# Moving ScalarE's first shifted copy ahead of the second unit's exponentials, with half the constant turns

## The chip, the cores and the metric

The kernel runs on one core of a Trainium2 chip. The metric is the time of one execution in microseconds (us), lower is better. A core has TensorE (PE in the profile, with PEld for its weight loads), VectorE (DVE), ScalarE (ACT), GpSimd (POOL) and SyncE (SP), which here only issues transfers.

## The reference

Sliding-window causal attention with a window of 64 over 8 batches, 8 heads, 576 positions and 64 dimensions a head, in float32, is followed by a mixture of 8 experts in which the expert of a token depends on the token before it.

```python
scores = scale * q @ k.T                      # mask: 0 <= pos_q - pos_k < 64
attn = softmax(where(mask, scores, -1e9))
x = (attn @ v) as [8, 576, 512]
# per token: fresh = argmax(x @ w_gate); gate = sigmoid(x @ w_local)
# e = fresh if first or gate < 0.5 else the expert of the token before
# out = softmax(logits)[e] * relu(x @ w1[e]) @ w2[e]
```

## The kernel before

The 4608 tokens are taken in 9 groups (`sc`) of 512 and each group in 4 head pairs (`hp`): a **unit** is one group and one head pair, and there are 36. The attention of all units comes first, up to about 131 us in the profile; then come the experts, with the matrix products of blocks of 256 tokens, up to the end. Between them, and partly beside the attention, the router's tables are built.

For a unit, `scores` (L378) makes 36 small matmuls into two PSUM tiles `sp` (each a weight load and a matmul of 64x128 from `w`, the tile of q and k; L385), then two exponentials on ScalarE into the SBUF tile `p` (L416), then one multiplication of `p` with a mask on VectorE (L421). `values` (L423) makes 32 matmuls from `p` with the value tiles `va` and `vb` into a PSUM pair `xo` (L431), and then VectorE takes a reciprocal (L436) and writes the scaled result `x` (L441). `sp` has three buffers, so the tiles of units 1, 2, 3, 4, 5 take buffers (0,1), (2,0), (1,2), (0,1), (2,0). `xo` has two pairs, used in turn.

`va` holds the values as they come from memory; `vb` holds them shifted by 64 rows, because windows cross the blocks of 128. For the first group `shift_first` (L369) makes `vb`, four heads at a time: GpSimd copies the lower rows (L375), ScalarE the upper ones (L376). Both need the transfer of that half of `va`. For later groups `shift` (L355) does the same in four steps (L360 to L367).

`warm(n)` (L245) puts n turns (transposes of the constant identity matrix) on TensorE, into a PSUM bank that nobody reads (L249). It stands twice: 12 turns at the start and 24 between the scores of the first two units and the values of the first.

The orders of TensorE, ScalarE and SyncE are the order in which the program is written (`manual_schedule`). VectorE's and GpSimd's are chosen ahead of time by a planner in the framework, with constraints such as `issue_after`, which holds the second mask's construction (`build_mask(1)`, L275) behind the multiplication that was traced last. All waits are semaphores that the framework places.

The start runs so: scores of units 1 and 2; `shift_first(0)`; the turns; then in the loop for i = 0 the values of unit 1, the scores of unit 3, `shift_first(1)`; for i = 1 the values of unit 2 and the scores of unit 4; for i = 2 the scores of unit 5 (the second group's first) and the values of unit 3; and so on, scores two units ahead. At i = 3 also eight turns of the first group's result, for the router (`turn`, L302).

The transfers of the second group (`load(1, ...)`, L228 and L233) are issued on SyncE behind `until(0, ...)` (L239), a tiny transfer that waits for the first mask; those of the third group behind a like one that waits for unit 1's reciprocal.

Of the kernel before, what the change touches and what calls it, by code (L numbers as in the profile page):

```python
# [83 lines left out]
def kernel(  # L84
# [37 lines left out]
    with ExitStack() as fast:  # L122
        ring = fast.enter_context(tc.tile_pool(name="ring", bufs=4))
        rt = Router(fast, tc, lt, xs, tabs, ident)
        ex = Experts(fast, tc, ring, *moe)
        zeros, n = ex.xp.tile([P, PITCH], F32, name="xg"), (ZR - T1) // HF
        nc.vector.memset(zeros[:HF], 0.0)
        for i in (ZR, N + 1):
            nc.gpsimd.dma_start(out=xs[i:i + 1, :], in_=zeros[:1])
        nc.gpsimd.dma_start(out=xs[T1:ZR, D:].rearrange("(c p) o -> p c o", p=HF),  # L130
                            in_=zeros[:HF, :n * (PITCH - D)].rearrange("p (c o) -> p c o", c=n))
        attention(tc, ring, kq, v3, v4, vt, vh, xs, lt, ok, wgs, wg2s, ident, rt, ex)
        ex.run(fast, rt, lambda ps: flag(nc, ps, ok, bad, tabs["ej"][:, NBLK:], rare, ident))
# [34 lines left out]
def attention(ctx, tc, ring, kq, v3, v4, vt, vh, xs, lt, ok, wg, wg2, ident, rt, ex):  # L168
# [31 lines left out]
    def bank():  # L200

        return ps_e.tile([P, SC], F32, name="r")
# [8 lines left out]
    def space(name, sc):  # L211
        return kp.tile([P, 4, H, width(sc)], F32, name=name, bufs=2 if name == "vb" else 3)
# [24 lines left out]
    def until(i, x):  # L237

        nc.sync.dma_start(out=late[:, i:i + 1], in_=x)  # L239
# [5 lines left out]
    def warm(n):  # L245

        r = bank()
        for _ in range(n):
            nc.tensor.transpose(r[:, :P], ident, ident)  # L249
# [20 lines left out]
    def build_mask(i):  # L270
        m = cp.tile([P, KB, 2, WIN], F32, name=f"mask{i}")
        for c in range(2):
            h = slice(c * WIN, (c + 1) * WIN)
            for par in range(2):
                nc.vector.tensor_scalar(m[h, :, par, :], colf[h], rowf[h], None, Alu.is_ge if par == c else Alu.is_lt)  # L275
        mid = MID[i]
        other = slice((1 - mid % 2) * WIN, (2 - mid % 2) * WIN)
        nc.vector.memset(m[other, mid // 2, mid % 2, :], 0.0)
        masks.append(m.rearrange("p a b q -> p (a b q)"))
# [89 lines left out]
    def shift_first(half):  # L369

        va, h = vas[0], slice(4 * half, 4 * half + 4)
        if not half:
            vbs[0] = space("vb", 0)
            nc.gpsimd.memset(vbs[0][WIN:, 0], 0.0)
        nc.gpsimd.tensor_copy(vbs[0][:WIN, :, h], va[:WIN, :, h])  # L375
        nc.scalar.copy(vbs[0][WIN:, 1:, h], va[WIN:, :3, h])  # L376
# [67 lines left out]
    units = [(sc, hp) for sc in range(NSC) for hp in range(HP)]  # L444
    ps = {}
    masked = []
    for u in units[:LEAD]:
        ps[u] = scores(*u)
    shift_first(0)
    with tc.issue_after(masked[-1].ins):  # L450
        build_mask(1)
    warm(24)
    until(0, masks[0][:1, :1])
    load(1, [pairs[0], whole, pairs[1]])
    moves, gated, turned, old = (), None, None, None
# [1152 lines left out]
```

## Time and profile before

| | |
|---|---|
| runs | 645.85, 646.2, 647.71 us; median 646.2 |
| profiled execution | 643.61 us, of it a span of 641.5 us and 2.1 us around it |
| TensorE, matmuls / weight loads busy in the span | 96% / 85% |
| VectorE / ScalarE / GpSimd busy | 63% / 31% / 20% |
| transfers | 166.43 MB; mean busy share of the DMA engines 0.75 to 1.02 by stretches of the first 60 us |
| TensorE idle, 0 to 160 us / 160 to 600 us | 16.8 us / 1.8 us |

The idle times of the last row are worked out from the table of stretches (length less the matmuls' busy time). Times are counted from the start of the span. A matmul's duration in the profile is longer than the distance to the next one, since they overlap: 32 matmuls of 0.22 us take 1.05 us together. In the idle column, a name behind the arrow is what the engine waited for by the profile; "issue" is a wait for nothing that the profile shows.

### The profile page before, as it was taken

The numbers are of one execution on the slowest core, as the hardware profiler recorded it, in microseconds if no ns is written. First come the engines' busy times: TensorE is split into PE (matmuls) and PEld (weight loads), VectorE is DVE, ScalarE is ACT, GpSimd is POOL, SyncE is SP. The second block draws the span as 40 slices with busy tenths as digits, with TensorE's granted clock in tenths as the row PEclk, the third lists the DMA queues.
The fourth block names the chain that finished last, engine by engine and source line by source line (L and its number), as shares of the span: only waits on it lengthen the run. The fifth ranks groups of instructions, "written<-read, shape, count | busy, mean of one in ns | idle before, by whom it ended". The sixth has DMA issues, their size and how long they took to land. (4 is left out here: it accounts for less than half of the span.)

```text
span 641.5 us, 14988 instructions
## 1 busy us (share of the span) xinstructions
PE 616.2 (96%) x6367; PEld 543.7 (85%) x6367; DVE 401.2 (63%) x752; ACT 200.9 (31%) x368; POOL 130.0 (20%) x132
## 2 busy tenths in 40 slices
PE   8888898989999999999999999999999999999995
PEld 7777766878889999978998999887997998899994
DVE  5676488879977775273553683363827653876730
ACT  3756655622572122112120313021211221122120
POOL 5322111330103202102312220221312022101101
PEclk9999999999999999999999999999999999999999
DMA  8988999989746655686957666679768556946501
GB/s 332 417 334 334 377 352 361 342 286 340 242 155 229 242 198 197 214 318 239 395 200 271 220 231 230 238 255 347 266 229 317 206 198 221 389 161 221 218 17 38
DMA packets 29318, 166.43 MB, mean 259 GB/s; under 512 B 8451, under 2 KB 9497, under 8 KB 20026
## 3 DMA queue, kind: packets, MB, share of 16 engines
q1 hardware_dynamic: 20394, 135.54, 58.2%
q0 software_dynamic: 8848, 29.85, 12.1%
q8 instruction: 52, 0.85, 0.5%
q14 instruction: 24, 0.20, 0.1%
HBM read 146.18 MB, written 19.59 MB: 258 GB/s over the span
## 5 line engine op out<-in xcount | busy, mean ns | idle before, releaser
L1387 POOL DMA_INDIRECT out_dram<-y,idx x36 | 42.4, 1178 | 344.3 <-DVE y L1323 196.8
L1314 PE MATMUL hp<-ws,hs 128*128 128x256 f32 x384 | 88.7, 380 | 0.0
L1314 PEld LDWEIGHTS hp<-ws,hs 128*128 128x128 f32 x384 | 72.6, 190 | 10.5 <-issue 0.8
L1264 PE MATMUL hp<-xs,ws 128*128 128x128 f32 x672 | 79.6, 275 | 0.0
L1264 PEld LDWEIGHTS hp<-xs,ws 128*128 128x128 f32 x672 | 77.3, 192 | 0.0
L1323 DVE SCALAR_TENSOR_TENSOR y<-hp,xg,kept 128x256 f32<-128x256 f32 x48 | 22.7, 482 | 74.9 <-issue 47.4
L1407 PE MATMUL hp<-xt,w 128*64 128x64 f32 (+2 forms) x640 | 66.2, 276 | 0.0
L1407 PEld LDWEIGHTS hp<-xt,w 128*128 128x128 f32 (+1 forms) x640 | 60.8, 170 | 4.1 <-issue 0.7
L1314 PE MATMUL hp<-w,h 128*128 128x256 f32 x256 | 61.1, 382 | 0.0
L1275 DVE TENSOR_TENSOR h<-hp,keep 128x512 f32<-128x512 f32 x42 | 28.7, 690 | 48.4 <-PE hp L1264 48.4
L1159 POOL DMA_INDIRECT xg<-xs,gx x40 | 48.2, 1204 | 42.5 <-issue 36.2
L1264 PEld LDWEIGHTS hp<-xt,w 128*128 128x128 f32 x448 | 53.2, 192 | 2.7 <-issue 1.3
L1264 PE MATMUL hp<-xt,w 128*128 128x128 f32 x448 | 54.7, 275 | 0.0
L1314 PEld LDWEIGHTS hp<-w,h 128*128 128x128 f32 x256 | 47.2, 190 | 6.3 <-issue 0.4
L416 ACT ACTIVATE p<-sp 128x512 f32<-128x512 f32 x72 | 39.2, 595 | 38.2 <-PE sp L385 36.1
L431 PE MATMUL xo<-vb,p 128*64 128x74 f32 (+1 forms) x576 | 44.2, 228 | 7.1 <-issue 4.0
L385 PEld LDWEIGHTS sp<-w 64*64 64x64 f32 x1296 | 38.5, 135 | 14.2 <-issue 10.8
L421 DVE TENSOR_TENSOR p<-p,mask 128x1024 f32<-128x1024 f32 x29 | 36.1, 1243 | 20.2 <-ACT p L416 20.1
L385 PE MATMUL sp<-w 64*64 64x128 f32 (+1 forms) x1296 | 44.0, 267 | 4.2 <-issue 3.5
L431 PEld LDWEIGHTS xo<-vb,p 128*64 128x64 f32 x576 | 38.4, 136 | 10.2 <-issue 5.3
L1276 ACT ACTIVATE h<-h 128x512 f32<-128x512 f32 x42 | 26.3, 630 | 59.1 <-DVE h L1275 59.1
L431 PE MATMUL xo<-va,p 128*64 128x74 f32 (+1 forms) x576 | 44.3, 228 | 0.2 <-issue 0.2
(280 smaller groups left out, 951.5 us busy)
## 6 DMA issues: line engine op xcount, KB each, us to landing
w<-in_w_dram SPq DMA_DIRECT2D x42, 2048.0 KB, 8.9
w<-in_kq_dram SPq DMA_DIRECT2D x17, 1024.0 KB, 9.8
w<-in_w_dram SPq DMA_DIRECT2D x24, 512.0 KB, 8.2
xs<-x POOLq DMA_DIRECT2D x9, 1024.0 KB, 11.4
va<-in_v_dram SPq DMA_DIRECT2D x5, 1184.0 KB
vtt<-in_vt_dram SPq DMA_DIRECT2D x5, 1024.0 KB
va<-in_v_dram SPq DMA_DIRECT2D x3, 1040.0 KB, 9.9
va<-in_v_dram SPq DMA_DIRECT2D x2, 520.0 KB, 7.7
```

Of the source, the lines that this page charges most:

```text
L385: nc.tensor.matmul(sp[j][c * WIN:(c + 1) * WIN, a:b], lhsT=kt[h, hp, block * WIN:(block + 1) * WIN], rhs=qt[h, hp, a:b], start=not biased, ...
L416: nc.scalar.activation(p[:, j], sp[j], Act.Exp, scale=DH ** -0.5)
L421: masked.append(nc.vector.tensor_tensor(p, p, m.to_broadcast([P, 2, SC]), op=Alu.mult))
L431: nc.tensor.matmul(xo[par * WIN:(par + 1) * WIN, j, s * VW:s * VW + n], lhsT=p[:, j, b * WIN:(b + 1) * WIN], rhs=w[:, s, 2 * hp + j, :n], ...
L1159: self.nc.gpsimd.indirect_dma_start(out=x, out_offset=None, in_=self.xs[:rows, :], in_offset=bass.IndirectOffsetOnAxis(ap=gx[:, s:s + 1], ...
L1264: nc.tensor.matmul(out[:, m, :], lhsT=a[:, kk, m * P:(m + 1) * P], rhs=b[:, kk, :], start=start and m + kk == 0, stop=stop and (m, kk) == ...
L1275: nc.vector.tensor_tensor(o, x, y, op=add)
L1276: nc.scalar.activation(o, x if y is None else o, Act.Relu)
L1314: nc.tensor.matmul(out, lhsT=a[:, m, :], rhs=b[:, m, :], start=start and m == 0, stop=stop and m == FK // 2 - 1, skip_group_check=True)
L1323: nc.vector.scalar_tensor_tensor(y[i][:, j * w:(j + 1) * w], x, pw[i], y2, Alu.mult, Alu.add)
L1387: self.nc.gpsimd.indirect_dma_start(out=self.out[:, :], out_offset=bass.IndirectOffsetOnAxis(ap=st["idx"][:, s:s + 1], axis=0), in_=y, in_ ...
L1407: nc.tensor.matmul(hp[a, i, :], lhsT=st["w1"][:, kk, m * P:(m + 1) * P][:, a], rhs=st["xt"][:, kk, :n], start=(kk == 0), stop=(kk == DK - 1))
```

## The change

ScalarE's order is changed: the copy of `shift_first(0)` is issued right after the first unit's two exponentials and ahead of the second unit's. GpSimd's two instructions of the same function are traced earlier too. On TensorE the second row of turns has 12 instead of 24 of them; every later TensorE instruction thus stands 24 records (12 weight loads and 12 matmuls) earlier in its stream.

```diff
     for u in units[:LEAD]:
         ps[u] = scores(*u)
-    shift_first(0)
+        if u == units[0]:
+            shift_first(0)
     with tc.issue_after(masked[-1].ins):
         build_mask(1)
-    warm(24)
+    warm(12)
     until(0, masks[0][:1, :1])
     load(1, [pairs[0], whole, pairs[1]])
```

## The prediction

> **What bounds the kernel now.** The engine table first: TensorE's matmuls are busy for 616 of 641.5 us. The table of stretches then says where the other 25 us lie: in 220 to 600 us TensorE idles 0.95 us of 380, but in 0 to 140 us it idles 16.8. So a saving counts only if TensorE is still early where the attention ends (131 us); from there its work is gapless and hands the lead to the end.
>
> The timelines of the engines around the change, TensorE's two lines first, then ScalarE, GpSimd and VectorE:
>
> ```profile
> 9.10 2.84 PE L249 MATMUL r<-ident 128*128 128x128 f32 x24
> 11.87 0.27 PE L431 MATMUL xo<-vb,p 128*64 128x65 f32 x1
> ...
> 9.23 1.09 ACT L416 ACTIVATE p<-sp 128x512 f32<-128x512 f32 x2 [0.73 <-PE sp L385]
> 10.34 0.84 ACT L376 COPY vb<-va 64x780 f32<-64x780 f32 x1
> ...
> 9.51 1.14 POOL L375 COPY vb<-va 64x1040 f32<-64x1040 f32 x1 [3.46 <-DMA va<-in_v_dram]
> ...
> 10.35 1.39 DVE L421 TENSOR_TENSOR p<-p,mask 128x1024 f32<-128x1024 f32 x1 [0.60 <-ACT p L416]
> 11.66 1.79 DVE L275 TENSOR_SCALAR mask<-p,rowf 64x512 f32<-64x512 f32 x4
> ```
>
> Unit 1's values start at 11.87, when the 24 turns end. Their inputs were there at 11.18 (ScalarE's copy, which stood behind unit 2's exponentials), 10.65 (GpSimd's copy) and 9.75 (unit 1's mask). So the turns bind by 0.7 us, behind them the copy.
>
> What TensorE meets next, and later in the attention:
>
> ```profile
> 16.35 0.40 PE L385 MATMUL sp<-w 64*64 64x128 f32 x2 [0.16 <-DMA w<-in_kq_dram]
> 16.92 1.11 PE L385 MATMUL sp<-w 64*64 64x128 f32 x34 [0.17 <-ACT p L416]
> ...
> 28.05 0.99 PE L385 MATMUL sp<-w 64*64 64x128 f32 x24 [0.69 <-issue]
> ...
> 39.70 0.27 PE L385 MATMUL sp<-w 64*64 64x64 f32 x2 [0.83 <-issue]
> ...
> 130.14 0.22 PE L431 MATMUL xo<-vb,p 128*64 128x74 f32 x1 [1.75 <-issue]
> ```
>
> Two walls. At 16.35 unit 5's scores wait for their q and k. And the "issue" pauses are regular: counted from the start of the trace, TensorE's records (loads, matmuls, semaphores) resume after a pause at numbers 705, 961, 1217, 1473, 1729, 1985, 3009, 4033 and 5313, that is 705 plus multiples of 256. The page's queue table has the cause:
>
> ```profile
> q8 instruction: 52, 0.85, 0.5%
> ```
>
> The columns are packets, MB and share of the engines. 0.85 MB in 52 is 16 KB, or 256 records of 64 bytes. In the trace such a transfer starts some 2.4 us before each of these resumptions (25.67 for the one at 28.05).
>
> [...] while the DMA engines are full, the transfer starts 3.3 to 4.7 us after a block was entered (in one case 1.25), and with the 2.4 us a block lasts no less than about 5.7 to 7.1 us: 21.05, 28.05, 33.97, 39.70, 46.81, 53.19 us. [...] the copy waited behind both exponentials though its input was there. [...] The 12 first turns took 2.82 us and the later 24 took 2.84, so the clock was up by 9.1; pauses of 1.75 us did not lower it.
>
> **The change part by part.**
> *The copy.* Its input lands at 9.5 by GpSimd's start. It runs 9.5 to 10.35 (0.84) instead of 10.34 to 11.18. Nothing bounds the landing from below but the end of unit 1's exponentials, 8.5; from above it has no bound: each us that it comes later is a us for unit 2's exponentials, which now stand behind it.
> *The turns.* 12 x (2.84/24) = 1.42 us, 9.10 to 10.52. Unit 1's values then wait for GpSimd's copy alone: 10.65, start 10.7. TensorE gains 11.87 - 10.7 = **1.17 us** here.
> *What is queued behind the moved copy.* Unit 2's exponentials go from 9.23 to 10.37 and end at 11.46 (+1.14). Their PSUM buffers are wanted by unit 3's scores at 11.85: free in time. Unit 2's mask runs 11.5 to 12.7; unit 2's values want it at 12.9: in time. VectorE's queue slips with it: second mask to 14.6, unit 1's reciprocal 14.6 (13.55 before), x to 15.5, unit 3's mask 15.5 (15.26 before, where VectorE had idled 0.84). So VectorE gives back all but 0.25 us, and at 19.26, after another idle 0.65, the rest. SyncE's third-group transfers follow unit 1's reciprocal, 1.1 us later; the DMA engines are at 1.02 of full up to 16 us and 1.01 up to 24, and of 6.2 MB issued for the first two groups about 5.1 have moved at 15.4 (256, 395 and 421 GB/s over 8, 4 and 3.4 us). With 1.1 MB queued they land no later: cost nothing. If that backlog were gone it would be 1.1 us on a transfer whose first reader is unit 9. GpSimd's copy keeps its time.
> *TensorE to the first wall.* Values 1, scores 3, values 2, scores 4 run without a pause from 10.7 and end at 15.1 (16.2 before). Scores 5 start at 16.35 as before, since the q and k were issued behind the first mask, untouched. But the second pause goes: unit 4's exponentials end by 16.25 (17.35 before). Scores 5 end at 17.5 instead of 18.0. **Left: 0.5 us.**
> *TensorE through the blocks.* At 21.05 the block pause was covered: unit 3's x, which frees a PSUM pair for unit 4's values, came at 21.75. That x is now some 0.4 us earlier, and so are the values. The block border lies 24 records further on in the work, ten records into unit 4's values, [...] at about 21.4 instead of 21.05: 0.4 us late. Against it, every border comes 24 records later in the work, worth 0.4 us where matmuls are dense (0.017 us a record) and up to 0.9 where slow turns lie between. From 28 to 53 us, where border follows border, this leaves 0 to 0.9 us. Past that, other waits rule, and the last border (130.14) would stand inside the last unit's values, 24 records in: 0.4 us.
> *Sum:* 1.17 - 0.67 (wall of q and k) = 0.5, less 0.4 for the late request, plus 0.4 for the records: **0.5 us gained**. The profiled execution would go from 643.61 to 643.1; the median of the runs stands 2.6 above that execution, so 645.7.
> *Bounds of what is not shown.* How the borders fall on some 19 blocks: pauses of 0.4 to 1.75 us, some 8 us in all; if each changes by half a us either way, independently, that is about 2 us in total as a wide estimate, and I take 1.2 as the likely size in either direction. The planner's order on VectorE and GpSimd: if unit 1's reciprocal went ahead of unit 2's mask, unit 2's values would start as before and the gain at the front be 0; from the other side 0.2. I take the order unchanged.
>
> **Rivals.** 0.3% (1.9 us) is about what a measurement of this kernel can tell from no change.
> *The pauses go (faster).* TensorE reaches borders early, and two or three of the larger pauses (0.8 to 1.75 us at 39.7, 46.8, 77.8, 101.9, 130.1) fall where it waits for ScalarE or VectorE anyway. For it: at 21.05 and 58.8 it was just so. Against: [...] being early moves the border too. With 1.2 at the front and 2 of them at 0.9 it gives 643.2.
> *The request behind a wait (slower).* Place: the border in unit 4's values. Each us by which their wait ends after 21.05 delays a chain of five blocks. If VectorE's slip of 1.1 us isn't absorbed, and the landing of va is 0.6 us later than in this profile, unit 3's x ends at 23.5, and the request leaves 2.4 us late, less 0.4 for the records; one more pause of the same form at the attention's end adds 0.4: 648.6. It decides from about 23.4 us on; below that it only eats the gain. For it: nothing in VectorE's order can overtake the second mask. Against: the idle 0.84 and 0.65.
> *Nothing happens.* The front is a wait for q and k either way; only the copy's place differs: 646.2, inside no change.
>
> **How the numbers follow.** The likeliest is a small gain, 645.7, with 644.4 to 647.1 from the borders; with "nothing happens" it has 0.56. Pauses go: 0.30. Request behind a wait: 0.14. As all within 0.3% falls in the first two, the chances are 0.30, 0.56, 0.14. For 8 in 10 the range takes in most of the faster case and the near end of the slower: 643.0 to 648.2.
>
> **What would show it.** After: unit 1's values at 10.7; ScalarE's copy at 9.5 and unit 2's exponentials at 10.4; scores 5 still at 16.35 with a longer wait for q and k, about 1.2 us, and no second pause; unit 3's mask at 15.5; pauses "issue" at the same record numbers, so later in the work; the last unit's values ending about 0.5 us before 131.2. Wrong would be: scores 5 starting well before 16.3, unit 3's x after 22, or a lead at 131 us of over 2 us.

## The result and the profile after

The changed kernel takes 648.2 us (median of 22 runs) and the kernel before, on the same chip, 646.07 (22 runs): a ratio of 1.0039 [1.0022, 1.0056], about 2.5 us slower. The profiled execution shows 649.37 us instead of 643.61. It overstates the loss: executions of one kernel differ by over 5 us (one kernel below was profiled at 648.89 and again at 643.24). Times are therefore judged by the timed runs, and a trace only says where a loss lies.

TensorE's busy time hardly changed, its idle time grew. The engine lines of the pages before and after:

```profile
PE 616.2 (96%) x6367; PEld 543.7 (85%) x6367; DVE 401.2 (63%) x752; ACT 200.9 (31%) x368; POOL 130.0 (20%) x132
PE 615.5 (95%) x6355; PEld 543.2 (84%) x6355; DVE 402.2 (62%) x752; ACT 200.9 (31%) x368; POOL 130.9 (20%) x132
```

The timeline of TensorE's matmuls after the change (start, length, line, operation; in brackets the idle time before it and what ended it):

```profile
8.60 1.53 PE L249 MATMUL r<-ident 128*128 128x128 f32 x12
10.80 0.27 PE L431 MATMUL xo<-vb,p 128*64 128x65 f32 x1 [0.67 <-POOL vb L375]
...
12.39 1.12 PE L385 MATMUL sp<-w 64*64 64x128 f32 x36 [0.44 <-DMA w<-in_kq_dram]
...
15.82 0.56 PE L385 MATMUL sp<-w 64*64 64x128 f32 x10 [0.21 <-issue]
16.65 1.52 PE L385 MATMUL sp<-w 64*64 64x128 f32 x36 [0.27 <-DMA w<-in_kq_dram]
18.09 0.27 PE L431 MATMUL xo<-vb,p 128*64 128x65 f32 x1
...
22.43 0.24 PE L431 MATMUL xo<-vb,p 128*64 128x65 f32 x1 [1.11 <-DVE x L441]
...
87.91 1.09 PE L385 MATMUL sp<-w 64*64 64x64 f32 x36
...
93.04 0.22 PE L431 MATMUL xo<-vb,p 128*64 128x74 f32 x1 [3.19 <-issue]
...
93.73 0.41 PE L400 MATMUL sp<-bias,unit 64*64 64x512 bf16 x4
94.01 1.08 PE L385 MATMUL sp<-w 64*64 64x64 f32 x34
```

The same places in the kernel before, unit 3's values and the two rows of scores about 91 us:

```profile
17.96 0.27 PE L431 MATMUL xo<-vb,p 128*64 128x65 f32 x1
...
88.94 1.09 PE L385 MATMUL sp<-w 64*64 64x64 f32 x36
...
91.31 0.41 PE L400 MATMUL sp<-bias,unit 64*64 64x512 bf16 x4
```

The gain at the front is there: unit 1's values start at 10.80 instead of 11.87, held by GpSimd's copy as forecast, and unit 5's scores still wait for q and k. By unit 3's values nothing of it is left (18.09, before 17.96). At 91 us there is a new pause of 3.19 us, "issue", in the middle of a unit's values. From one row of scores to the next (87.91 to 93.73) TensorE takes 5.8 us; the kernel before takes 2.4 for the same work, without a pause.

The other engines at the front, ScalarE, GpSimd and VectorE:

```profile
9.67 0.84 ACT L376 COPY vb<-va 64x780 f32<-64x780 f32 x1 [1.68 <-DMA va<-in_v_dram]
10.54 1.08 ACT L416 ACTIVATE p<-sp 128x512 f32<-128x512 f32 x2
...
13.76 1.34 POOL L375 COPY vb<-va 64x1040 f32<-64x1040 f32 x1 [3.01 <-DMA va<-in_v_dram]
...
12.80 2.58 DVE L275 TENSOR_SCALAR mask<-p,rowf 64x512 f32<-64x512 f32 x4
15.48 0.14 DVE L436 RECIPROCAL allr<-xo 128x8 f32<-128x8 f32 x1
...
21.59 0.69 DVE L441 TENSOR_TENSOR x<-xo,allr 128x512 f32<-128x512 f32 x1
```

The copy starts when its data lands, and the exponentials follow. The second mask takes 2.58 us instead of 1.79, with a GpSimd copy in the middle of it; unit 1's reciprocal comes at 15.48 (13.55 before, 14.6 forecast).

### The profile page after: what moved, and what is told of

It reads as the page before. It is cut to its first block, busy times and chain, and to the rows that moved or that the text cites. A ratio compares the mean times of both kernels' runs of the same rounds, so it can differ in the third digit from the quotient of the medians.

```text
span 647.2 us, 14964 instructions
## 1 busy us (share of the span) xinstructions
PE 615.5 (95%) x6355; PEld 543.2 (84%) x6355; DVE 402.2 (62%) x752; ACT 200.9 (31%) x368; POOL 130.9 (20%) x132
## 5 line engine op out<-in xcount | busy, mean ns | idle before, releaser
L1388 POOL DMA_INDIRECT out_dram<-y,idx x36 | 40.0, 1111 | 344.2 <-DVE y L1324 198.3
L1315 PEld LDWEIGHTS hp<-ws,hs 128*128 128x128 f32 x384 | 72.6, 190 | 10.5 <-issue 0.8
L1160 POOL DMA_INDIRECT xg<-xs,gx x40 | 50.1, 1252 | 43.8 <-issue 37.9
L1315 PEld LDWEIGHTS hp<-w,h 128*128 128x128 f32 x256 | 47.2, 190 | 6.3 <-issue 0.4
L385 PEld LDWEIGHTS sp<-w 64*64 64x64 f32 x1296 | 37.7, 134 | 14.2 <-issue 10.4
## 6 DMA issues: line engine op xcount, KB each, us to landing
xs<-x POOLq DMA_DIRECT2D x9, 1024.0 KB, 10.7
```

Of the source, the lines that this page charges most:

```text
L385: nc.tensor.matmul(sp[j][c * WIN:(c + 1) * WIN, a:b], lhsT=kt[h, hp, block * WIN:(block + 1) * WIN], rhs=qt[h, hp, a:b], start=not biased, ...
L1160: self.nc.gpsimd.indirect_dma_start(out=x, out_offset=None, in_=self.xs[:rows, :], in_offset=bass.IndirectOffsetOnAxis(ap=gx[:, s:s + 1], ...
L1315: nc.tensor.matmul(out, lhsT=a[:, m, :], rhs=b[:, m, :], start=start and m == 0, stop=stop and m == FK // 2 - 1, skip_group_check=True)
L1388: self.nc.gpsimd.indirect_dma_start(out=self.out[:, :], out_offset=bass.IndirectOffsetOnAxis(ap=st["idx"][:, s:s + 1], axis=0), in_=y, in_ ...
```

## The experiments

Each kernel was timed in five rounds beside the kernel before. Two theories stood against each other: **the front** (ScalarE's and VectorE's slip delays the attention; the expectations call it the slip) and **the borders** (in the traces of before and after every "issue" pause of over 0.55 us between two of TensorE's records stands at a record number of 449 plus a multiple of 256; these numbers are the borders and what lies between two of them a block, and with 24 records fewer every border falls elsewhere in the work). "Shifted" below means that the work behind the front stands 24 records earlier than before, "unshifted" that it stands where it stood.

**1. The two halves.** `copy_only` has the moved copy with `warm(24)`; `turns_only` has `shift_first(0)` where it was.

```diff
# turns_only
-    warm(24)
+    warm(12)
```

> The moved copy with all 24 turns, so that every later TensorE record keeps its old number. Border theory (the 24 records by which the instruction blocks' borders move cost the time): TensorE's stream is as before, so 0 to +0.5 us against the kernel before, and the record behind which TensorE pauses at about 91 us shows no pause over 1 us. Slip theory (the second unit's exponentials, and with them VectorE's queue, come 1.1 us later and never recover): +2 us or more, as with the whole change.

> 12 turns instead of 24, the copy where it was. Border theory: +1.5 to +3 us, since all later records stand 24 earlier, with a pause of over 1 us at about 91 us in the trace. Slip theory: no loss, rather a gain of up to 0.7 us, since unit 1's values start at about 11.2 instead of 11.87 us and VectorE's queue isn't late.

Measured: copy alone 1.0012 [0.9983, 1.0041], and repeated on another chip

> The moved copy with all 24 turns, run again for a narrower interval. Borders alone: 0 to +0.5 us. If the late exponentials cost by themselves: +1 us or more.

0.999 [0.997, 1.0011]: the moved copy costs nothing that can be measured. Turns alone: 1.0052 [1.0032, 1.0072]. The loss comes from 12 turns fewer. The traces at 91 us, first `copy_only`, then `turns_only`:

```profile
88.05 1.09 PE L385 MATMUL sp<-w 64*64 64x64 f32 x36
90.41 0.41 PE L400 MATMUL sp<-bias,unit 64*64 64x512 bf16 x4
```

```profile
89.82 0.22 PE L431 MATMUL xo<-vb,p 128*64 128x74 f32 x1 [1.29 <-issue]
```

With 24 turns the two rows of scores are 2.4 us apart as before. With 12 the pause is back, at the same record.

**2. Time or records?** Twelve turns fewer are both 1.4 us less of TensorE's time and 24 records less. Wide matmuls in place of turns were to separate the two.

```diff
# shortened; n is 12 in wide_turns, 6 in wide_six
-    warm(24)
+    r = bank()
+    for _ in range(n):
+        nc.tensor.matmul(r[:, :2 * P], lhsT=ident,
+                         rhs=kts[0][:, 0, :2 * P], start=True, stop=True)
```

> The kernel before with its 24 turns replaced by 12 matmuls of twice the width (about 2.6 us in all instead of 2.84): almost the same start, but every later record 24 earlier. Border theory: +1.5 to +3 us with nothing else changed. Slip theory: the time of before within 0.3 us.

This one missed its purpose. TensorE's timeline:

```profile
9.09 5.45 PE L456 MATMUL r<-w,ident 128*128 128x256 f32 x24
14.47 0.27 PE L431 MATMUL xo<-vb,p 128*64 128x65 f32 x1
```

Twelve such matmuls are 24 records of matmuls and 24 of loads, so the numbers did not move, and they take 5.45 us instead of 2.84. It tells something else: unit 1's values start 2.6 us late, and the kernel takes 1.0022 [1.0004, 1.004]. By the medians even 2.6 us at the front cost less than the change does, though the intervals overlap. Six of them are then the test that was meant: the front's time unchanged (values at 11.88), 24 records fewer, the copy where it was.

> The kernel before with its 24 turns replaced by 6 matmuls of 128x256, which the earlier run showed to be two records of matmul each and some 0.22 us a record: 2.7 us in all for the 2.84 of the turns, and 24 records fewer. Border theory: +1.3 to +3 us and a pause of over 1 us at about 91 us, with nothing else changed. Slip theory: the time of before within 0.5 us.

Measured: 1.0031 [1.0013, 1.005]. Fewer records alone, with the front's time kept and no engine's order changed, make a loss of this size. The pause and what follows it in the trace of `wide_six`:

```profile
92.95 0.22 PE L431 MATMUL xo<-vb,p 128*64 128x74 f32 x1 [3.19 <-issue]
...
94.49 1.95 PE L385 MATMUL sp<-w 64*64 64x64 f32 x34
```

The same row of 34 matmuls takes 1.95 us here and 1.08 in the changed kernel. By the table of stretches the granted clock was lowered to 0.50 from about 93.1 to 96.5 us, behind this pause; half of these 3.4 us, about another 1.7 us, is the estimate of what it cost.

**3. The records put back.** Twelve turns more ahead of unit 5's scores, where TensorE waits for q and k: the front stays short, and from 16 us on every number is as before.

```diff
         if 1 < i < len(units) - LEAD:
+            if i == 2:
+                warm(12)
```

> The whole change, and 12 turns put back ahead of unit 5's scores, where TensorE waits for q and k: from there on every record has its old number. Border theory: the loss goes, -0.5 to +0.5 us against the kernel before. Slip theory: +2 us or more, as with the whole change, as the front is the same.

> The kernel before with 12 of its 24 turns moved from ahead of unit 1's values to ahead of unit 5's scores; the copy stays where it was. From unit 5 on every record has its old number. Border theory: -0.7 to +0.7 us. If what the turns are placed between matters instead (an early TensorE is harmful by itself): +1.5 us or more, as with 12 turns only.

`turns_late` (copy unmoved): 1.0013 [0.9999, 1.0027]. `late_turns` (whole change): 1.0028 [1.0007, 1.0049], which is no clear return.

**4. The slip taken away.** In `mask_late` the second mask stands behind unit 1's `x` on VectorE (`values` now returns that instruction), so that the slip ends there; `mask_late_turns` has the turns of 3 too.

```diff
-    with tc.issue_after(masked[-1].ins):
-        build_mask(1)
...
+        done = values(sc, hp, ps.pop((sc, hp)), x, g)
+        if i == 0:
+            with tc.issue_after(done.ins):
+                build_mask(1)
```

> The whole change, with the second mask built behind unit 1's result on VectorE instead of ahead of it, so that unit 1's and unit 3's results and the third group's transfers come some 2.5 us earlier than in the changed kernel. Slip theory: the loss of the change goes, 0 to +0.7 us against the kernel before. Border theory: it stays at +1.5 to +3 us, since the records keep the numbers of the changed kernel.

> Both repairs: the second mask behind unit 1's result, and 12 turns put back ahead of unit 5's scores. If the loss is the sum of borders and slip: -1 to +0.5 us against the kernel before. If neither carries it: +1 us or more.

Without the slip but shifted: 1.0045 [1.002, 1.0071]. Without it and unshifted: 0.9996 [0.998, 1.0011]. So the slip isn't what costs the time. Whether it explains why `late_turns` did not return fully stays open: the intervals of the two overlap.

**5. Half the shift.** `turns_18` is the kernel before with 12 records fewer.

```diff
-    warm(24)
+    warm(18)
```

> 18 turns instead of 24, the copy where it was: records 12 earlier, so the router's wait stands 77 records behind the border instead of 89 (24 turns, no pause) or 65 (12 turns, pause). If the place of the request is below 77 records: no pause at 91 us and -0.7 to +0.5 us. If it is above: a pause of over 0.7 us there and +1.3 to +3 us. A loss that grew with each missing turn alone would give about half of that of 12 turns, +1.5 us, with no pause at 91 us.

1.0013 [0.9992, 1.0034], and no pause at 91 us. The one trace doesn't decide on the place of the request: the next block's transfer started 0.4 us behind this block's first record, ahead of the router's wait, and from 89.41 us on the clock was at 0.50 for 3.4 us: the pairs of matmuls of a row of values stand 0.12 us apart there, against 0.065 in the row ahead of it, and the block is the longer for it.

**6. Where in the attention?** A suspect was the router's wait for `loc` (TensorE's L819 of the kernel before, at 87 us). Small turns (32x32, 24 records, 0.52 us) were put ahead of that wait to move the border back: right ahead of it (`router_turns`, on the change, and `wide_six_router`, on `wide_six`), or ahead of the router's first turn of `vk` (`wide_early`, `after_early`, `turns_early`). `wide_behind` has the same turns behind the wait, as the counterpart.

```diff
# router_turns, wide_six_router: ahead of the turns of loc and thru
+        if not part:
+            r = psum()
+            for _ in range(12):
+                nc.tensor.transpose(r[:32, :32], ident[:32, :32], ident[:32, :32])
# the three "early" kernels; wide_behind has the same lines behind the turns of loc and thru
+        bk = psum()
+        if not part:
+            for _ in range(12):
+                nc.tensor.transpose(bk[:32, 2 * P:2 * P + 32],
+                                    ident[:32, :32], ident[:32, :32])
-        tp = psum()[:n, :2 * P].rearrange("c (i p) -> c i p", i=2)
+        tp = bk[:n, :2 * P].rearrange("c (i p) -> c i p", i=2)
```

> The whole change, and 12 small turns (32x32, 24 records) put ahead of the router's product of loc, which waits for VectorE at 86 us. So only from there on do the records have their old numbers; everything earlier is as in the changed kernel. If the one border at 91 us carries the loss (the request for its block standing behind that wait): no pause over 0.5 us at 91 us, and 0 to +1 us against the kernel before. If the shift of all the earlier borders carries it: +1.5 to +3 us still.

> The kernel before with 6 wide matmuls in place of its 24 turns (24 records fewer, copy unmoved), and the 12 small turns ahead of the router's product of loc. One border at 91 us: no pause there, -0.3 to +0.7 us against the kernel before, where the same without the small turns was 1.0031. All borders: +1.3 us or more.

`router_turns` 1.003 [1.0014, 1.0046], `wide_six_router` 1.0032 [1.0018, 1.0047]. They missed: the pause stays (`router_turns`, below). By the author's reading the small turns, in their own bank, have a wait of their own at the very record that was to be freed:

```profile
90.98 0.22 PE L431 MATMUL xo<-vb,p 128*64 128x74 f32 x1 [1.68 <-issue]
```

> Six wide matmuls in place of the 24 turns (24 records fewer), and 12 small turns ahead of the router's first turn (vk), behind the wait that this turn has anyway. The wait for loc then stands 89 records behind the border again. If the request behind that wait carries the loss: no pause at 91 us, and -0.7 to +0.7 us against the kernel before (1.0031 without the small turns). If earlier borders carry it: +1.3 us or more.

> The same with the 12 small turns about 100 records later, right behind the router's products of loc and thru: the wait stays 65 records behind the border, all later records have their old numbers. If the request behind the wait carries the loss: a pause of over 0.7 us at 91 us, and +1.3 to +3 us. If it was borders after 91 us: the time of before within 0.7 us.

> The whole change with the 12 small turns ahead of the router's first turn. If the request behind the wait carries the loss: no pause at 91 us, and the loss of 2.5 us falls to -0.5 to +1 us. If not: +1.5 us or more.

> 12 turns with the copy unmoved, and the 12 small turns ahead of the router's first turn. If the request behind the wait carries the loss: no pause at 91 us; the shifted records left TensorE some 1 to 2 us earlier at 60 us in the traces of shifted kernels, so -1.5 to +0.5 us against the kernel before, the best candidate. If not: +2 us or more, as with 12 turns only.

`wide_early` 1.0043 [1.002, 1.0067], `wide_behind` 1.0049 [1.003, 1.0068], `after_early` 1.0044 [1.0029, 1.0059], `turns_early` 1.0031 [1.0015, 1.0048]. Putting the records back at this wait brings no return, and ahead of it is no better than behind it. But this doesn't show that the loss lies elsewhere, since the pause was not taken away: `after_early` has it with 1.3 us and `turns_early` with 0.7, although the wait for `loc` stands at its old number there. In `wide_early` and `wide_behind` it is missing, but there the clock was at 0.50 for 3.4 us within this block (some 1.7 us lost, by the same estimate), and that the longer block covered the next transfer for this reason is the author's reading.

**7. Controls.** The kernel before against itself, and the change again.

> The kernel before against itself. If the comparison is sound: a ratio within 0.2% of 1, and no pause at the border of 91 us. If it comes out at 0.3% or more from 1, all the differences of this study are within the noise.

> The change again on the same chip. If its loss is its own: +0.2 to +0.6%, with a pause of over 0.7 us at 91 us as in its first trace. If the loss came from the chip or the day: within 0.2%.

1.0002 [0.9985, 1.0019] and 1.0031 [1.0013, 1.005].

**What they show together.** The five kernels shifted through the whole program (the change twice, `turns_only`, `wide_six`, `mask_late`) have ratios of 1.0031 to 1.0052, mean 1.0040. The six unshifted (`copy_only` twice, `turns_late`, `late_turns`, `mask_late_turns`, the kernel before again) have 0.999 to 1.0028, mean 1.0007. The difference of 0.33% is 2.1 us. (`wide_turns`, unshifted too but 2.6 us late at the front, is left out; its 1.0022 would make the mean 1.0009.)

Where it lies was read by aligning the traces by TensorE's records, without the turns and wide matmuls. The points are named by their times in the kernel before; the last stands some 3 us ahead of the end of the attention's last values, which the trace shows at 134.5 us and not at 131, where the prediction put it. Mean lengths in us:

| stretch | unshifted (7 traces) | shifted (5 traces) |
|---|---|---|
| 11.9 to 59 us | 47.2 | 46.9 |
| 59 to 79 | 19.1 (18.2 to 20.5) | 20.3 (19.2 to 23.6) |
| 79 to 86 | 8.1 | 8.1 |
| 86 to 97 | 10.1 (10.0 to 10.5) | 12.6 (10.9 to 14.8) |
| 97 to 131.1 | 35.6 | 35.0 |

(The 7 are the kernel before and the six above.) Part of the loss is lowered clock. With the lost time of those stretches taken out, 59 to 79 us is 19.7 against 19.1, and 86 to 97 us is 10.9 to 13.4 in the shifted against 10.0 to 10.5 in the unshifted. In these traces the loss lies mainly in 86 to 97 us. At the border there, TensorE pauses for 0.7 to 3.4 us between records in all five shifted traces and in none of the seven.

Ahead of the end of this pause the queue of instructions (q8, 16 KB a transfer) has a transfer: in the changed kernel it starts at 90.71, and TensorE resumes at 93.04. Taken as the next block's, it starts, against the end of the router's wait for `loc`:

| kernel | wait ends | transfer starts | pause between records |
|---|---|---|---|
| before | 87.0 | 85.3 | 0 |
| copy_only | 86.1 | 86.8 | 0 |
| turns_only | 84.6 | 87.5 | 1.5 |
| mask_late | 86.2 | 88.2 | 1.0 |
| changed | 86.0 | 90.7 | 3.4 |
| changed, second trace | 90.5 | 92.4 | 0.7 |
| wide_six | 85.9 | 90.4 | 3.4 |

The expectations suspected a request that leaves some 65 to 77 records into a block and now stands behind the wait for `loc`. (Counted from the border in the order of start, this wait stands 81 records behind it in the unshifted kernels, 69 in `turns_18` and 57 in the shifted ones, each 8 less than they say.) The traces speak against such a place: in the kernel before, the transfer starts 41 records into this block, and in `wide_six` at 100.31 us, behind 0.8 us in which the DMA engines were idle (their share is 0.00 from 98 to 100 us), 18 records and 0.3 us into its block.

Another reading needs no request that is held back. The wait ahead of the router's turn of `vk`, first before, then after:

```profile
84.73 0.39 PE L809 MATMUL r<-ident,vk 128*14 128x128 f32 x2 [0.55 <-ACT va L348]
```

```profile
83.69 0.39 PE L810 MATMUL r<-ident,vk 128*14 128x128 f32 x2 [0.55 <-ACT va L348]
```

The block that ends at the pause begins at 83.88 us before and at 84.13 after. So this wait, 5 records behind the block's border in the unshifted kernels, stands 19 records ahead of it in the shifted ones and lengthens the block before instead. From its first record to its last the block takes 6.2 to 6.4 us in the seven unshifted traces and 5.3 to 5.5 in the five shifted ones. The next block's transfer starts 1.3 to 3.8 us behind the first record in the former, 3.8 to 6.6 in the latter, and where TensorE paused it resumed 2.3 to 2.6 us after that start. As an estimate from these figures, a transfer that starts 3.8 us into the block and is followed by work 2.6 us later is just covered by 6.4 us of work and not by 5.5. In all the kernels of 6 this wait (or the first small turn in its place) still stands ahead of the border, which would be why they did not get their time back. This fits the traces, but no run tests it, and why the transfers start later in the shifted traces stays open.

## Why the prediction was wrong

It gave 645.7 us and a small gain as the likeliest; the loss of 2.5 us had a chance of 0.14.

- **The front: right.** Values at 10.80 (10.7 forecast), held by GpSimd's copy; exponentials at 10.54 (10.4); no second pause in unit 5's scores (the second trace of the change has one of 0.68 us). "12 x (2.84/24) = 1.42 us" was read as 1.53 by the modelled end.
- **The wall of q and k: its place right, the way to it wrong.** Scores 5 start at 16.65 (16.35 forecast), but behind a wait of 0.27 us and not 1.2. That the rows ahead of them "run without a pause from 10.7 and end at 15.1" failed: unit 3's scores waited 0.44 us for their own q and k, and the border at record 449, which no pause showed in the kernel before, now falls into unit 4's scores and stops TensorE between records for 0.48 us (1.68 in the second trace of the change). So the "0.5 us" that was to be left was gone by unit 3's values: they start at 18.09 and 18.51 us in the two traces of the change, at 17.96 and 17.55 in those of the kernel before. A shorter front brought nothing that these runs can measure: `mask_late_turns`, which has it with the later records unshifted, is at 0.9996, and `wide_turns`, 2.6 us late there, loses only 0.2%.
- **VectorE's slip: a size that was off.** "second mask to 14.6" took the mask at 1.79 us; it took 2.58, and unit 3's x came at 21.59 to 22.28 where about 21.4 was forecast. The trace of one execution hid how this varies. The first half of `va` was copied from 8.3 us on in some traces and 9.7 in others, and where GpSimd's second copy falls inside the mask the mask takes 2.5 to 2.7 us, in the kernel before too (2.67, second trace). Beside a copy of 1.05 to 1.3 us the mask grows by 0.7 to 0.9; by what mechanism, no run here shows. This term did not decide: `mask_late` without the slip is as slow.
- **Third-group transfers, "cost nothing": not so in the first trace.** ScalarE's copy L363 waited 1.00 us for that `va` there, until 27.76; in the second trace of the change it starts at 26.63 without a wait.
- **The records: the step that failed.** The sum's "plus 0.4 for the records", with "1.2 as the likely size in either direction", treated the borders as noise around a small gain. `wide_six` measures the term alone: 1.0031, a loss of 2.0 us, and shifted against unshifted kernels give 2.1. The forecast reasoned that every border "comes 24 records later in the work" and priced the pauses that it could see. It left out the borders that showed none, such as those at record 449 and at 91 us, and did not ask how much work, waits included, each block would newly hold to cover the next transfer. Right was that the pauses stay at their record numbers: the new one of 3.19 us stands at 3521, which is 449 plus 12 times 256. How far a wait puts off the next block's transfer was the author's estimate, and no run tests it.
- **The rival "The request behind a wait": the sign and the kind are right, the place is wrong.** It named the border in unit 4's values, to decide from 23.4 us. Unit 3's x ended at 22.28, and by 59 us the shifted kernels are level. The new pause stands at 91 us, behind the router. That a wait holds back the request there is not shown; a block with less work in it explains the pause as well.
- **"Pauses of 1.75 us did not lower" the clock** was true of that trace (granted clock 1.00 from 8 to 600 us) and not of all: it fell to 0.50 in others, in `wide_early` behind a stretch with less idle time than that (see the last section).

What stays open: which borders carry the 2.1 us in the timed runs, and by which mechanism. Some 2 us lie in 86 to 97 us in the traces; 59 to 79 us may have a part, and there the ranges overlap. Lowered clock has a part too. The time lost to it, as an estimate (one less the granted clock, times the length of the timed run), is on average 1.2 us more than in the kernel before beside it in four of the shifted kernels (for the first timing of the change the clocks beside it are not on record), and 0.4 us more in the six unshifted. No version here was measurably faster than the kernel before.

## What to carry to other kernels

Where an engine's instruction stream stalls at regular record numbers, adding or removing instructions far upstream moves every later border, and this can cost more than the removed work was worth: here 24 records fewer cost 2.1 us, where values 1 started 1.07 us earlier. Ask of each block how much work and waiting it holds to cover the next one's transfer, also where no pause shows (here 6.2 to 6.4 us without a pause, 5.3 to 5.5 with one). Test it with a kernel that changes the count of records and nothing else. The gain in front of a wait for a transfer was worth nothing that these runs can measure (`mask_late_turns`, 0.9996). Before trusting a slip that is read from one trace, look at a second trace of the same kernel: here landings moved by over 1 us and a mask's length by half.

## What was not expected of the hardware

- One fp32 matmul of 128x256 gives two loads and two matmuls in the trace and takes 5.45/12 = 0.45 us; a turn of 128x128 gives one of each and takes 0.12. They are no replacement for each other when records are counted.
- In the first 140 us the granted clock fell to 0.50 for about 3.4 us at a time (6.8 us, two of them in a row, in the second trace of the change). 2 of the 7 unshifted traces and 3 of the 5 shifted ones have one or two such stretches. One came behind the 3.19 us pause of `wide_six` (about 1.7 us lost, as estimated above), but none behind the equally long one of the changed kernel, whose clock was at 1.00 there. Another came in `wide_early` at 86.47 us, where the matmuls had been busy for 2.25 of the 3.41 us before. What sets it off is not shown.
- Kernels that differ in nothing reach the point at 131.1 us up to 5 us apart in single traces (128.6 and 133.7 for `copy_only`), so one pair of traces can't show a difference of 2 us.
